# Linear attention and two feed-forward layers on one core: a Strassen-like slot opens the next slot's first product before it closes its own, and the written order is reckoned with other TensorE lengths

## The chip, the cores and the metric

The kernel runs on one core of one Trainium2 chip. Times are device microseconds (us) of that core, from the start to the end of one execution. Time before: median 829.05 us of three runs, which lie between 828.7 and 829.67. A difference under 0.2% (1.66 us) cannot be told from no change here.

## The reference

```python
kv  = einsum('bhsd,bhse->bhde', k, v)         # per batch and head: k^T v, 64 x 64
out = einsum('bhsd,bhde->bhse', q, kv)        # q, k, v: (4, 8, 576, 64)
x   = out / sqrt(mean(out*out, -1) + 1e-6) * g_norm
x   = x.transpose(0, 2, 1, 3).reshape(2304, 512)
x   = softplus(x @ w_in)  @ w_out            # moe:  w_in (512, 2048), w_out (2048, 512)
out = elu(x @ w_in2)      @ w_out2           # moe2: the same shapes
```

Everything is in float32.

## The kernel before

Each fp32 operand of a big product is split in two fp32r halves (`hi`, `lo`), and a product of two matrices is three matmuls (hi·hi, lo·hi, hi·lo). A matmul has 128 rows of contraction, 128 rows of output and 384 or 512 columns.

**Slots.** The 2304 tokens are six blocks of T = 384, taken in three pairs. The 2048 hidden columns are 16 chunks of 128, taken in four quarters. A layer has 4 quarters x 3 pairs x 2 chunk pairs = 24 slots; a slot makes the hidden values of one chunk pair for one pair of blocks (`slot_plain`, `slot_h`), and its results, split, are the tiles `G`. The product with `w_out` (`slot_out`, lines 986 to 988) runs in *pieces* of three matmuls, 384 wide in layer 0 and 512 wide in layer 1, for slots that are done; its banks are `acc`, and VectorE adds them up (`block_sum`, lines 570 to 584).

The first six slots multiply plainly (`plain_product`, line 759): four pairs of 6-matmul products. All later slots (`slot_h`) use seven products of six 384-wide matmuls (`product`, line 731) in place of eight. Products 1, 6, 7 and 4 add up in bank `A` (tag `h`, two banks). Between them ScalarE or VectorE copies what stands in `A` so far (`copy`, lines 819 and 821): `ca` after product 1, `cb` after 6, `cc` after 7, and the next product on `A` waits for its copy. Product 5 opens bank `B` (tag `m`, **one** bank), VectorE adds it into `cc` (`c22`, line 829), then product 3 closes `B`, and VectorE adds `B` into the copy `cb` (`c12`, line 829, `hj<-hj,B`), which frees the bank. Product 2 fills bank `C` (tag `o`) and is added into `ca` (`c11`). The activations follow (`slot_act`, lines 796 and 901 to 948).

**What sets the order.** All engines' instructions are written out in one order that the program works out when it is built. `Order.run` (lines 100 on) keeps strands, each with a key (how soon it is due) and a next step with a price per engine and what it needs; among the strands that could go next on an engine it takes the one with the smallest start time plus `min((key - least) * SLOPE, WAIT)`. The prices of TensorE's work come from `pe(n, passes)`. TensorE's slots and pieces are one strand, `main`, whose order inside a slot is the table `PRODUCTS`: numbers are products, words are counts of pieces. While nothing else of TensorE's is ready in the first slots, the strand `warm` (lines 1085 to 1100) issues 128 x 128 fp32 matmuls on an identity or a zero tile, which add nothing to the result and fill the time. An engine then runs its instructions strictly as written.

**The start.** Batches 0 to 3 of the attention (`kv` line 418, `po` line 481, transposes `pt` line 552) run on TensorE between the plain slots of the first 150 us; their inputs come by DMA, and VectorE, ScalarE and GpSimd work on them on the way to the split x. Weights are split on ScalarE and VectorE through the whole run (lines 282 to 357), and x tiles that are used again are written to DRAM (`spill`, line 701) and read back (line 688).

Of the kernel before, what the change touches and what calls it, by code (L numbers as in the profile page):

```python
# [1 line left out]

# [14 lines left out]
P = 128  # L17
# [7 lines left out]


def pe(n, passes=1):
    return passes * n * 0.4514 + 1


def act(n, psum=False):
# [11 lines left out]
class Order:  # L43
# [16 lines left out]

    COLD = 7300

    SLOPE = 60
    WAIT = 300
    EARLY_WAIT = 200
    def __init__(self):
        self.free = dict.fromkeys((PE, ACT, DVE, POOL, DMA), 0.0)
        self.marks = {}
# [99 lines left out]
def linear_attention_then_two_ffns(  # L168
# [27 lines left out]
    KC = DM // P  # L196
# [8 lines left out]
    NPAIR = NB // 2  # L205
    FP = QF // 2
    SLOTS = NQ * NPAIR * FP
    LAYERS = 2

    OPS = ((1, 6, 7, 5, 4, 2, 3), (1, 5, 6, 2, 7, 4, 3))  # L210
    PLAIN_OPS = (1, 2, 8, 4)
    EPS = 1e-6

# [11 lines left out]
    def ring(tag, n=1):  # L225
        return ("ring", tag, n)
# [176 lines left out]
    def kv_strand(b, c):  # L403
        n, r = 4 * 2 * D2, S - 4 * P
        yield ((DMA, dma(4 * n * P)),), room_free(KV_AT[b][c], b, c)
        t = acc_sb[KV_AT[b][c]]
        nc.sync.dma_start(t[:, :n], kv[b, c].rearrange("p n t d -> p (n t d)"))
        yield ((DMA, dma(2 * D2 * 4 * r)),), []
        nc.sync.dma_start(t[:r, n : n + 2 * D2], kv_rest[b, c].rearrange("p t d -> p (t d)"))
        old = [("po", x) for x in made_of(b - 2, c)] if b > 1 else []  # L410
        tag = "om"[c % 2]
        yield ((PE, 5 * 130),), [ring(tag), *old]
        p, p_h = psum(tag, f"kv{b}_{c}")
        for n in range(5):
            r = min(P, S - n * P)
            o = n * 2 * D2
            for i in range(2):
                nc.tensor.matmul(  # L418
                    p[i * D : (i + 1) * D, :D],
                    t[:r, o + i * D : o + (i + 1) * D],  # L420
                    t[:r, o + D2 + i * D : o + D2 + (i + 1) * D],
                    start=(n == 0),
                    stop=(n == 4),
                )
        mark("kvmm", b, c)
        f = kvf[b % 2][:, c, :]
        for i in range(2):
            s = slice(i * D, (i + 1) * D)
            e = yield ((ACT, act(D, True)), (DVE, dve(D))), []
            if e == ACT:  # L430
                nc.scalar.copy(f[s, s], p[s, :D])
            else:
                nc.vector.tensor_copy(f[s, s], p[s, :D])
        drop(p_h)
        mark("kv", b, c)
# [15 lines left out]
    def attention(nm):  # L451


        first = isinstance(nm, tuple)
        if first:
            j, c = nm
            products = [
                (b, c, slice(s, e), slice(i * D2, (i + 1) * D2), j * TT + i)
                for i in range(TT)
                for b, s, e in batches(j * TT + i)  # L460
            ]
            n = T
            x = acc_sb[j][:, c * T : (c + 1) * T]
            tag = "acc"
        else:
            j, o = divmod(nm, TT)
            products = [
                (b, c, slice(s, e), slice(c * D2, (c + 1) * D2), nm)
                for b, s, e in batches(nm)
                for c in range(NP)  # L470
            ]
            n = DM
            x = acc_sb[j].rearrange("p (c t) -> p c t", c=KC)[:, :, o * P : (o + 1) * P]
            tag = "acc" if j < 3 else "om"[nm % 2]
        h = n // D
        need = dict.fromkeys([("kv", p[0], p[1]) for p in products] + [("tile", p[4]) for p in products])

        yield ((PE, sum(pe(P, 4) for _ in products)),), [ring(tag), *need, *room_free(j, B, 0)]
        bank, po_h = psum(tag, f"po{nm}")
        for b, c, rows, cols, t in products:  # L480
            nc.tensor.matmul(  # L481
                bank[rows, cols], tile_q[t][0][:, c, rows], kvf[b % 2][:, c, :], start=True, stop=True
            )
        if first:
            drop(tile_q[products[0][4]][1])
        mark("po", nm)
        po = bank[:, :n]
        if not first:
            yield from late(nm, bank, po_h, x, tag)
            return  # L490
        yield ((ACT, act(n, True)),), [ring("e")]
        y, y_h = sbuf("e", 3, f"y{nm}", (P, 2, T))
        y = y.rearrange("p a b -> p (a b)")[:, :n]
        nc.scalar.activation(y, po, AF.Square, scale=D**-0.5)
        yield ((DVE, dve(n)),), [ring("small")]
        small, small_h = sbuf("small", 4, f"small{nm}", (P, 2, H))
        ms, r = (small[:, i, :h] for i in range(2))
        nc.vector.reduce_sum(ms, y.rearrange("p (h e) -> p h e", h=h), axis=AX.X)

        yield ((POOL, power(h)),), [("minus_half",)]  # L500
        root(r, ms)
        yield ((DVE, dve(n)),), []
        nc.vector.tensor_mul(
            y.rearrange("p (h e) -> p h e", h=h),
            po.rearrange("p (h e) -> p h e", h=h),
            r.unsqueeze(2).to_broadcast([P, h, D]),
        )
        drop(small_h)
        yield ((PE, n // P * 109),), [("ident",)]
        for i in range(n // P):  # L510
            s = slice(i * P, (i + 1) * P)
            nc.tensor.transpose(bank[:, s], y[:, s], ident)
        drop(y_h)
        yield ((ACT, act(n, True) + 90),), [("gn",)]
        nc.scalar.activation(x, po, AF.Copy, scale=gn)
        drop(po_h)
        mark("x", nm)
# [6 lines left out]
    def late(t, bank, po_h, x, tag):  # L524
# [20 lines left out]
        )  # L545
        drop(small_h)
        drop(po_h)
        yield ((PE, KC * 109),), [("ident",), ring(tag)]
        bank, po_h = psum(tag, f"pt{t}")
        for k in range(KC):  # L550
            s = slice(k * P, (k + 1) * P)
# [245 lines left out]
            drop(bank_h)  # L797
        yield from slot_parts(s, b, h, 2 * s + b)

    def slot_h(s, pieces):  # L800

        layer, q, p, f = slots[s]
        key = base(s)

        wide = s > FP and slots[s - FP][0] == 0
        k = {}

        def share(part):
            return {"all": 99, "half": 8 if wide else 6, "more": 3 if wide else 2, "one": 1, "two": 2}[part]

        def copy(name, tag, n, col):
            def strand():
# [21 lines left out]
            k[name] = psum(tag, f"{name}{s}", uses)  # L834
            return k[name][0]

        def some(n):
            yield from some_of(pieces, n)

        def first():  # L840
            yield from product(s, 1, lambda: open_("h", "A"), True, False, [ring("h")])
            chain[:] = [k["A"][0]]
# [6 lines left out]
        def seventh():  # L849
            yield from product(s, 7, k["A"][0], False, False, [("cb", s)])  # L850
            order.add(key - URGENT, copy("cc", "hk", 7, 1))

        def fifth():
            yield from product(s, 5, lambda: open_("m", "B"), True, False, [ring("m")])
# [12 lines left out]
        def third():  # L867
            yield from product(s, 3, k["B"][0], False, True, [("c22", s)])
            order.add(key - URGENT, add_to("hj", 1, *k["B"], "c12", []))
            order.add(key + H_KEY + 1, slot_act(s, 0, k["hj"], None))  # L870

        for step in PRODUCTS[layer]:
            if step in (1, 2, 3, 4, 5, 6, 7):
                yield from (first, second, third, fourth, fifth, sixth, seventh)[step - 1]()
            else:
                yield from some(share(step))
        if p == NPAIR - 1:
            for fc in (2 * f, 2 * f + 1):
                for h in w_t[layer, fc, 0][2:]:
                    drop(h)  # L880
            drop(wx_t[layer, 2 * f][1])

    def G_tiles(n, name):

# [83 lines left out]
    def slot_piece(layer, q, p, b, u, k, cut, acc, left):  # L968
# [29 lines left out]

    SUM_KEY = 0
    H_KEY = 2
    URGENT = 3
    X_LEAD = 3
    W_LEAD = 4
    W_LEAD2 = 8
    KV_KEY = (-20, -18, -5, 2)
    UNIT_KEY = (-19.9, -17.9, -9, -4, 4, 5)
    W_IN_FIRST = (-18.5, -11)
    W_OUT_FIRST = (-3, -1)  # L1010
    X_KEY = (-19, 2, 8)
    X_SUMS = (1.5, 9, 17)
    SPILL = 1
    WARM_SLOTS = 7
    FILLED = 8
# [2 lines left out]

    chain = []

    PRODUCTS = (
        (1, "more", 6, "more", 7, "one", 5, "more", 4, "one", 2, "more", 3, "two"),
        (1, 5, 6, 2, 7, "half", 4, 3, "all"),
    )

    class Pieces:
# [12 lines left out]
        def ready(self):  # L1039
            if not self:  # L1040
                return 0.0
            at = [order.when(n) for n in self.head[2]]
            return None if None in at else max(at)

        def take(self):
            if self:
# [8 lines left out]
    def some_of(pieces, n):  # L1055
        for _ in range(n):
            yield from one(pieces)
# [9 lines left out]
    def main():  # L1067
        groups = LAYERS * SLOTS // FP
        for g in range(groups):
            layer, q, p, _ = slots[FP * g]  # L1070
            for b in range(2):
                last = g == groups - 1 and b == 0
                pieces_of[FP * (g + 1) + (1 - b if g >= NPAIR else b)] = Pieces(slot_out(layer, q, p, b, last))
        for s in range(LAYERS * SLOTS + 2):
            if s:
                entry[0] = base(s)
            left = pieces_of.get(s, Pieces(iter(())))
            if s < FP * NPAIR:
                yield from slot_plain(s, left)
            elif s < LAYERS * SLOTS:  # L1080
                yield from slot_h(s, left)
            while left:
                yield from one(left)

# [124 lines left out]
```

## Time and profile before

| | before |
|---|---|
| median of 3 runs | 829.05 us |
| the profiled execution | 828.14 us |
| its span (first to last instruction) | 826.2 us |
| PE (TensorE matmul) busy | 819.5 us, 99% |
| PEld (weight loads, beside PE) | 773.9 us, 94% |
| DVE (VectorE) | 551.6 us, 67% |
| ACT (ScalarE) | 448.4 us, 54% |
| POOL (GpSimd) | 43.8 us, 5% |
| chain that ended last | PE 95%, ACT 2%, DVE 1%, POOL 1% |

A row of a timeline is: start, duration, engine, line, operation, output <- inputs, shape, count, and in brackets how long the engine had stood idle before it and what ended that. Matmuls overlap: the row of one lasts longer than the distance to the start of the next, which is the *pitch*, and the pitch is what a matmul costs in a row of matmuls. A tile's name is given without its numbers.

### The profile page before, as it was taken

The page shows a single profiled execution, that of the slowest core. Times are in us where ns is not written, and L with a number is a line of the kernel's source. Part 1 is how long each engine was busy: PE and PEld are TensorE (multiplying, and loading weights), DVE is VectorE, ACT ScalarE, POOL GpSimd, SP SyncE. Part 2 cuts the span into 40 slices and gives each one's busy share as a digit, 9 for nine tenths or more (in the row PEclk, how much of TensorE's full clock was granted, in tenths as well). Part 3 has the DMA queues.
Part 4 walks back from the last instruction along what each step waited for, and adds up shares of the span by engine and source line. Part 5 has one row for each costly group of instructions (what it writes and reads, how often), then busy time and mean ns, then how long its engine had stood idle before and what let it go on. Part 6 is the DMA issues. An engine that isn't in the chain of part 4 may idle for free.

```text
span 826.2 us, 12278 instructions
## 1 busy us (share of the span) xinstructions
PE 819.5 (99%) x4772; PEld 773.9 (94%) x4772; DVE 551.6 (67%) x906; ACT 448.4 (54%) x767; POOL 43.8 (5%) x47
## 2 busy tenths in 40 slices
PE   9999999999999999999999999999999999999998
PEld 8899999999999999999999998889889889889897
DVE  3787697354476565766399987767578766865444
ACT  4686785463255534544276777675364564563340
POOL 3442420000000000000000000000000000000000
PEclk9999999999999999999999999999999999999999
DMA  8988666774574674675644756673763763653713
GB/s 310 306 328 319 220 233 228 299 280 172 185 280 163 245 270 140 253 260 168 235 160 159 292 201 240 273 275 141 273 240 118 297 251 138 256 222 111 278 39 114
DMA packets 42537, 185.34 MB, mean 224 GB/s; under 512 B 4976, under 2 KB 6256, under 8 KB 42480
## 3 DMA queue, kind: packets, MB, share of 16 engines
q1 hardware_dynamic: 42480, 184.57, 60.8%
q8 instruction: 37, 0.61, 0.3%
q14 instruction: 20, 0.16, 0.1%
HBM read 146.80 MB, written 37.75 MB: 223 GB/s over the span
## 4 chain that ended last, share of the span: by engine, by line
PE 95%; ACT 2%; DVE 1%; POOL 1%; issue 0%; DVEq 0%
PE A L731 21%; PE acc L988 16%; PE acc L987 16%; PE acc L986 15%; PE B L731 10%; PE A L759 6%; PE C L731 5%; PE kv L418 2%; PE warm L1098 2%; PE po L481 1%; PE A L1098 1%; POOL small L522 1%; PE pt L552 1%; ACT acc_sb L570 0%; DVE x L693 0%
## 5 line engine op out<-in xcount | busy, mean ns | idle before, releaser
L986 PE MATMUL acc<-G,whi 128*128 128x384 f32 x384 | 128.7, 335 | 0.0
L988 PE MATMUL acc<-G,whi 128*128 128x384 f32 x384 | 128.3, 334 | 0.0
L987 PE MATMUL acc<-G,wlo 128*128 128x384 f32 x384 | 128.3, 334 | 0.0
L988 PE MATMUL acc<-wlo,G 128*128 128x512 f32 (+1 forms) x292 | 113.6, 389 | 0.0
L987 PE MATMUL acc<-whi,G 128*128 128x512 f32 (+1 forms) x292 | 113.5, 389 | 0.0
L986 PE MATMUL acc<-whi,G 128*128 128x512 f32 (+1 forms) x292 | 112.7, 386 | 0.0
L731 PE MATMUL A<-x,wx 128*128 128x384 f32 x504 | 101.3, 335 | 0.4 <-ACT hj L819 0.3
L731 PE MATMUL A<-x,whi 128*128 128x384 f32 x336 | 99.5, 337 | 0.4 <-ACT hk L796 0.4
L731 PEld LDWEIGHTS A<-x,wx 128*128 128x128 f32 x504 | 88.5, 188 | 1.4 <-ACT hj L819 1.4
L986 PEld LDWEIGHTS acc<-G,whi 128*128 128x128 f32 x384 | 72.1, 188 | 0.1
L987 PEld LDWEIGHTS acc<-G,wlo 128*128 128x128 f32 x384 | 72.1, 188 | 0.0
L988 PEld LDWEIGHTS acc<-G,whi 128*128 128x128 f32 x384 | 72.1, 188 | 0.0
L576 DVE TENSOR_TENSOR acc_sb<-acc_sb,acc 128x384 f32<-128x384 f32 (+1 forms) x108 | 62.1, 597 | 12.5 <-PE acc L988 12.5
L988 PEld LDWEIGHTS acc<-wlo,G 128*128 128x128 f32 x292 | 54.8, 188 | 11.2
L731 PEld LDWEIGHTS A<-x,whi 128*128 128x128 f32 x336 | 62.4, 188 | 2.5 <-ACT hk L796 0.8
L987 PEld LDWEIGHTS acc<-whi,G 128*128 128x128 f32 x292 | 54.8, 188 | 10.3
L986 PEld LDWEIGHTS acc<-whi,G 128*128 128x128 f32 x292 | 54.9, 188 | 10.2
L312 ACT CAST whi<-q 128x512 fp32r<-128x512 f32 x64 | 39.7, 620 | 41.7 <-DVE q L341 12.4
L819 ACT COPY hj<-A 128x384 f32<-128x384 f32 x56 | 26.9, 480 | 61.2 <-PE A L731 61.2
L316 DVE TENSOR_TENSOR wlo<-q,whi 128x512 fp32r<-128x512 f32 x64 | 44.0, 688 | 23.3 <-ACT whi L312 23.2
L829 DVE TENSOR_TENSOR hj<-hj,B 128x384 f32<-128x384 f32 x42 | 23.2, 553 | 53.0 <-PE B L731 53.0
L829 DVE TENSOR_TENSOR hk<-hk,B 128x384 f32<-128x384 f32 x42 | 23.3, 554 | 52.2 <-PE B L731 37.6
(169 smaller groups left out, 1604.1 us busy)
## 6 DMA issues: line engine op xcount, KB each, us to landing
x<-spill SPq DMA_DIRECT2D x126, 768.0 KB, 6.3
raw<-w SPq DMA_DIRECT2D x64, 512.0 KB, 6.5
spill<-x SPq DMA_DIRECT2D x42, 768.0 KB, 4.6
acc_sb<-kv SPq DMA_DIRECT2D x16, 512.0 KB, 5.6
q<-qt SPq DMA_DIRECT2D x18, 256.0 KB, 4.9
out<-o SPq DMA_DIRECT2D x17, 256.0 KB, 2.1
acc_sb<-kv_rest SPq DMA_DIRECT2D x16, 64.0 KB, 5.3
out<-o SPq DMA_DIRECT2D x2, 128.0 KB, 1.7
```

The costliest lines, as they stand in the source:

```text
L312: nc.scalar.copy(hi, q)
L316: nc.vector.tensor_sub(lo, q, f32(hi))
L418: nc.tensor.matmul(p[i * D : (i + 1) * D, :D], t[:r, o + i * D : o + (i + 1) * D], t[:r, o + D2 + i * D : o + D2 + (i + 1) * D], start=(n ...
L576: nc.vector.tensor_add(a, a, p)
L731: nc.tensor.matmul(bank[:, :T], w, x, start=start and i == 0, stop=stop and i == len(seq) - 1, skip_group_check=True,)
L759: nc.tensor.matmul(a[:, :T], w, x, start=half == 0 and i == 0, stop=half == 1 and i == len(seq) - 1, skip_group_check=True,)
L819: nc.scalar.copy(to, a[:, :T])
L829: nc.vector.tensor_add(to, to, bank[:, :T])
L986: nc.tensor.matmul(a, l[0], r[0], start=(u == 0), stop=False)
L987: nc.tensor.matmul(a, l[1], r[0], start=False, stop=False)
L988: nc.tensor.matmul(a, l[0], r[1], start=False, stop=(u == QF - 1))
L1098: nc.tensor.matmul((chain[0] if chain else p)[:, -P:], a, a, start=not chain, stop=not chain, skip_group_check=True)
```

## The change

There are three parts.

1. **Product 1 of the next slot comes early.** `slot_h` gives back its seven steps in place of running them, and `main` holds the steps of this slot and of the next. The table `STEPS` takes the place of `PRODUCTS`: a 1 there means the *next* slot's product 1, which now stands ahead of products 4 and 3 of this slot. The order of a slot's other products becomes 6, 5, 2, 7.
2. **One run of 512-wide pieces a slot.** In layer 1 a slot had two runs of pieces (`"half"` and `"all"`). Now it has one, of 6 pieces in even slots and 18 in odd ones; the pieces that an even slot leaves are kept and go ahead of the odd slot's (`Pieces.follow`).
3. **Other numbers for the order.** `pe` goes from 174.3 to 173.3 ns for 384 columns, from 232.1 to 226.6 for 512 and from 232.1 to 263.3 for the filler's four passes of 128; transposes, `kv`, the slopes, waits and keys change too. These numbers set the order alone.

```diff
 def pe(n, passes=1):
-    return passes * n * 0.4514 + 1
+    return passes * n / 2.4 + (13.3 if passes == 1 else 50)
...
-    SLOPE = 60
-    WAIT = 300
-    EARLY_WAIT = 200
+    SLOPE = 90.0
+    WAIT = 118.0
+    EARLY_WAIT = 190.0
...
-    OPS = ((1, 6, 7, 5, 4, 2, 3), (1, 5, 6, 2, 7, 4, 3))
+    OPS = ((1, 6, 5, 2, 7, 4, 3),) * 2
...
-        yield ((PE, 5 * 130),), [ring(tag), *old]
+        yield ((PE, 880),), [ring(tag), *old]
...
-    def slot_h(s, pieces):
+    def slot_h(s):
...
         def seventh():
             yield from product(s, 7, k["A"][0], False, False, [("cb", s)])
             order.add(key - URGENT, copy("cc", "hk", 7, 1))
+            if p == NPAIR - 1:
+                drop(wx_t[layer, 2 * f][1])
...
-        for step in PRODUCTS[layer]:
-            if step in (1, 2, 3, 4, 5, 6, 7):
-                yield from (first, second, third, fourth, fifth, sixth, seventh)[step - 1]()
-            else:
-                yield from some(share(step))
-        if p == NPAIR - 1:
...
+        return None, first, second, third, fourth, fifth, sixth, seventh
...
-    SUM_KEY = 0
-    H_KEY = 2
-    URGENT = 3
+    SUM_KEY = -1.52
+    H_KEY = 1
+    URGENT = 8
...
-    PRODUCTS = (
-        (1, "more", 6, "more", 7, "one", 5, "more", 4, "one", 2, "more", 3, "two"),
-        (1, 5, 6, 2, 7, "half", 4, 3, "all"),
+    STEPS = (
+        ((6, "4", 5, 2, "4", 7, "8", 1, 4, 3),) * 2,
+        ((6, 5, 2, 7, "6", 1, 4, 3), (6, 5, 2, 7, "18", 1, 4, 3)),
     )
...
+        def follow(self, other):
+            self.pieces = itertools.chain(self.pieces, other.pieces)
...
             left = pieces_of.get(s, Pieces(iter(())))
+            if kept:
+                kept.follow(left)
+                left, kept = kept, None
             if s < FP * NPAIR:
                 yield from slot_plain(s, left)
             elif s < LAYERS * SLOTS:
-                yield from slot_h(s, left)
+                if s == FP * NPAIR:
+                    now = slot_h(s)
+                    yield from now[1]()
+                for step in STEPS[slots[s][0]][s % FP]:
+                    if isinstance(step, str):
+                        yield from some_of(left, int(step))
+                    elif step > 1:
+                        yield from now[step]()
+                    elif s + 1 < LAYERS * SLOTS:
+                        then = slot_h(s + 1)
+                        yield from then[1]()
+                now = then
+                if slots[s][0] and s % FP == 0:
+                    left, kept = kept, left
             while left:
                 yield from one(left)
```

The first place is on TensorE, at the start of plain slot 1 (`A_0_0`, block 1's first product), with the attention and the filler ahead of it (`A_1_1` is the last bank of slot 0, onto which the filler multiplies the identity with `start` and `stop` off). Before:

```order
L1098 MATMUL A_1_1_647<-ident 128x128 x4
L481 MATMUL po_722<-kvf_69,q_466 128x128 x4
L481 MATMUL po_733<-kvf_69,q_499 128x128 x4
L1098 MATMUL A_1_1_647<-ident 128x128 x9
L759 MATMUL A_0_0_768<-x_0_0_1_299,whi_2_0_560 128x384
L759 MATMUL A_0_0_768<-x_0_0_1_299,wlo_2_0_589 128x384
```

and after:

```order
L760 MATMUL A_1_1_615<-x_0_0_4_557,whi_1_0_387 128x384 x2
L553 MATMUL pt_638<-ident,q_395 128x128 x4
L419 MATMUL kv_2_646<-acc_sb_75 64x64 x10
L553 MATMUL pt_661<-ident,q_395 128x128 x4
L760 MATMUL A_0_0_669<-x_0_0_1_289,whi_2_0_498 128x384
L760 MATMUL A_0_0_669<-x_0_0_1_289,wlo_2_0_522 128x384
```

Here the fillers ahead of slot 1 are gone and the `po` products of the next batch come later. Counted over the whole order, there are 70 rows' worth of fillers before (42 ahead of the first plain product, 28 behind it) and 34 after (32 and 2); one such matmul is two records in the trace, so 140 records before and 68 after.

The second place is on TensorE too, in layer 1, around product 3, which closes bank `B` (the only one of its tag). Before, the last products of a slot (`A_5788`, `B_5799`) are followed by its 18 matmuls on `acc` (the first three are shown) and then by the next slot's product 1, so product 5 reopens bank `B` 24 matmuls behind product 3:

```order
L731 MATMUL A_5788<-x_1_1_4_5630,whi_7_0_5384 128x384 x2
L731 MATMUL B_5799<-x_1_1_3_5653,whi_7_0_5384 128x384
L731 MATMUL B_5799<-x_1_1_3_5653,wlo_7_0_5394 128x384
L731 MATMUL B_5799<-x_1_1_3_5653,whi_7_0_5384 128x384
L731 MATMUL B_5799<-x_1_1_3_5653,wlo_7_0_5394 128x384
L731 MATMUL B_5799<-x_1_1_3_5653,whi_7_0_5384 128x384 x2
L986 MATMUL acc_1_0_0_0_5840<-whi_6_1_5574,G_0_5666 128x512
L987 MATMUL acc_1_0_0_0_5840<-whi_6_1_5574,G_0_5666 128x512
L988 MATMUL acc_1_0_0_0_5840<-wlo_6_1_5579,G_0_5666 128x512
```

and after, where `A_5867` and `B_5902` are the next slot's banks:

```order
L732 MATMUL A_5712<-x_1_1_4_5623,wlo_7_0_5286 128x384
L732 MATMUL A_5712<-x_1_1_4_5623,whi_7_0_5280 128x384 x2
L732 MATMUL B_5759<-x_1_1_3_5649,whi_7_0_5280 128x384
L732 MATMUL B_5759<-x_1_1_3_5649,wlo_7_0_5286 128x384
L732 MATMUL B_5759<-x_1_1_3_5649,whi_7_0_5280 128x384
L732 MATMUL B_5759<-x_1_1_3_5649,wlo_7_0_5286 128x384
L732 MATMUL B_5759<-x_1_1_3_5649,whi_7_0_5280 128x384 x2
L732 MATMUL A_5867<-x_1_2_6_5778,wx_4_5106 128x384 x6
L732 MATMUL B_5902<-x_1_2_5_5803,wx_4_5106 128x384 x6
```

The next slot's product 1 now stands ahead of these rows, its product 6 follows product 3 at once, and product 5 (`B_5902`) comes only 6 matmuls behind product 3 of the last slot (`B_5759`).

The third place is on VectorE at the same point of a layer 1 slot, around `c12`, the add `hj<-hj,B` that frees that bank; `c`, `r`, `raw`, `q` are steps of the split of a weight tile. Before:

```order
L295 ISA q_9_0_5782<-c_9_0_5781,r_9_0_5795 128x1024
L288 TENSOR_SCALAR c_10_0_5861<-c_10_0_5861 128x512
L290 SCALAR_TENSOR_TENSOR c_10_0_5861<-raw_10_0_5741,c_10_0_5861 128x512
L295 ISA q_10_0_5862<-c_10_0_5861,r_10_0_5867 128x1024
L829 TENSOR_TENSOR hj_5808<-hj_5808,B_5799 128x384
L920 SCALAR_TENSOR_TENSOR hk_5844<-e_1_5889,A_5788 128x384
L925 SCALAR_TENSOR_TENSOR hk_5844<-e_1_5889,hk_5844 128x384
```

and after:

```order
L359 TENSOR_TENSOR wx_10_6105<-t_1_10_6107,wx_10_6105 128x256
L289 TENSOR_SCALAR c_10_1_6143<-c_10_1_6143 128x512
L291 SCALAR_TENSOR_TENSOR c_10_1_6143<-raw_10_1_5757,c_10_1_6143 128x512
L826 TENSOR_TENSOR hj_5990<-hj_5990,B_6016 128x384
L296 ISA q_10_1_6144<-c_10_1_6143,r_10_1_6167 128x1024
L818 COPY hj_6165<-A_6150 128x384
```

Ahead of `c12` stand steps of a weight's split in both; behind it now comes another step of the split and a copy of the next slot's bank `A`, where there were steps of the slot's own activation.

## Rows read from the trace of the kernel before

**Rows 1.** Windows: busy us (count) by engine, granted clock, DMA share, GB/s.

```profile
25.00:57.00 32.00, 32.00 (x316) 29.08 (x315) 25.63 (x43) 24.26 (x50) 16.50 (x16) 1.00 0.92 322
150.58:431.80 281.22, 281.22 (x1622) 281.22 (x1623) 168.27 (x295) 132.50 (x225) 0.00 (x0) 1.00 0.60 217
560.00:826.00 266.00, 263.13 (x1318) 236.79 (x1316) 171.13 (x278) 122.96 (x200) 0.00 (x0) 1.00 0.50 189
```

**Rows 2.** Line 1098, the filler: records, min/median/max ns, first and last start.

```profile
L1098 PE MATMUL A<-ident x56: 271/275/377, 31.6 to 56.3; 128*128 128x128 f32 x56
L1098 PE MATMUL warm<-kvf x42: 275/326/582, 1.4 to 13.2; 128*128 128x128 f32 x42
L1098 PE MATMUL warm<-ident x42: 275/275/377, 15.3 to 23.9; 128*128 128x128 f32 x42
```

**Rows 3.** Timeline of TensorE, runs of filler and the start of slot 1.

```profile
1.44 4.21 PE L1098 MATMUL warm<-kvf 128*128 128x128 f32 x18 [1.44 <-DVE kvf L1113]
...
54.44 2.17 PE L1098 MATMUL A<-ident 128*128 128x128 f32 x18
56.57 0.44 PE L759 MATMUL A<-x,whi 128*128 128x384 f32 x1
```

**Rows 4.** Timeline of ScalarE, the last softplus of slot 0.

```profile
56.02 0.50 ACT L796 ACTIVATE hk<-A 128x384 f32<-128x384 f32 x1
```

**Rows 5.** Waits of TensorE in the first 151 us: total, times, longest.

```profile
PE pt L552 <- DVE q L541: 0.9, 2, 0.6
PE A L731 <- ACT hk L796: 0.4, 1, 0.4
```

**Rows 6.** Timeline of TensorE: two layer 1 slots begin; two 512-wide pieces.

```profile
572.90 0.33 PE L731 MATMUL A<-x,whi 128*128 128x384 f32 x1
...
588.47 0.33 PE L731 MATMUL A<-x,whi 128*128 128x384 f32 x1
...
811.26 0.39 PE L986 MATMUL acc<-whi,G 128*128 128x512 f32 x1
...
816.02 0.39 PE L986 MATMUL acc<-whi,G 128*128 128x512 f32 x1
```

**Rows 7.** Timeline, layer 1, TensorE and ScalarE: first and last stops at product 7.

```profile
497.51 0.51 PE L731 MATMUL C<-x,whi 128*128 128x384 f32 x2
497.79 0.47 ACT L819 COPY hj<-A 128x384 f32<-128x384 f32 x1
...
498.31 1.32 PE L731 MATMUL A<-x,wx 128*128 128x384 f32 x6 [0.29 <-ACT hj L819]
...
529.66 0.51 PE L731 MATMUL C<-x,whi 128*128 128x384 f32 x2
530.24 0.97 PE L731 MATMUL A<-x,wx 128*128 128x384 f32 x4
```

**Rows 8.** Timeline: product 3 and the add that frees its bank; product 5.

```profile
429.58 0.51 PE L731 MATMUL B<-x,whi 128*128 128x384 f32 x2
...
431.64 0.55 DVE L829 TENSOR_TENSOR hj<-hj,B 128x384 f32<-128x384 f32 x1
...
432.24 0.45 PE L731 MATMUL B<-x,wx 128*128 128x384 f32 x1
...
584.00 0.51 PE L731 MATMUL B<-x,whi 128*128 128x384 f32 x2
...
584.55 0.55 DVE L829 TENSOR_TENSOR hj<-hj,B 128x384 f32<-128x384 f32 x1 [1.85 <-PE B L731]
```

**Rows 9.** The page, part 6: reloads of x, KB each, median us to landing.

```profile
x<-spill SPq DMA_DIRECT2D x126, 768.0 KB, 6.3
```

**Rows 10.** Timeline: from a slot's last product on A to its G.

```profile
583.51 0.49 ACT L911 ACTIVATE e<-A 128x384 f32<-128x384 f32 x1 [2.26 <-PE A L731]
...
586.81 0.82 ACT L946 CAST G<-hk 128x768 fp32r<-128x768 f32 x1
...
589.28 0.95 DVE L948 TENSOR_TENSOR G<-hk,G 128x768 fp32r<-128x768 f32 x1
```

More of the change, by code (lines that the diff above doesn't have):

```diff
@@ L1 @@
+import itertools
 from contextlib import ExitStack
@@ L508, in attention @@
         drop(small_h)
-        yield ((PE, n // P * 109),), [("ident",)]
+        yield ((PE, n // P * 90),), [("ident",)]
         for i in range(n // P):
@@ L547, in late @@
         drop(po_h)
-        yield ((PE, KC * 109),), [("ident",), ring(tag)]
+        yield ((PE, KC * 90),), [("ident",), ring(tag)]
         bank, po_h = psum(tag, f"pt{t}")
@@ L798, in plain_act @@
         yield from slot_parts(s, b, h, 2 * s + b)
-    def slot_h(s, pieces):
+    def slot_h(s):
         layer, q, p, f = slots[s]
         key = base(s)
-        wide = s > FP and slots[s - FP][0] == 0
         k = {}
-        def share(part):
-            return {"all": 99, "half": 8 if wide else 6, "more": 3 if wide else 2, "one": 1, "two": 2}[part]
         def copy(name, tag, n, col):
@@ L835, in open_ @@
             return k[name][0]
-        def some(n):
-            yield from some_of(pieces, n)
         def first():
@@ L870, in third @@
             order.add(key + H_KEY + 1, slot_act(s, 0, k["hj"], None))
-        for step in PRODUCTS[layer]:
-            if step in (1, 2, 3, 4, 5, 6, 7):
-                yield from (first, second, third, fourth, fifth, sixth, seventh)[step - 1]()
-            else:
-                yield from some(share(step))
-        if p == NPAIR - 1:
[L878 to L881, printed above, removed]
+            if p == NPAIR - 1:
+                for fc in (2 * f, 2 * f + 1):
+                    for h in w_t[layer, fc, 0][2:]:
+                        drop(h)
+        return None, first, second, third, fourth, fifth, sixth, seventh
     def G_tiles(n, name):
@@ L997, in slot_piece @@
             order.add(base(s) + SUM_KEY, block_sum(layer, q, 2 * p + b, i, w0, w1, *acc.pop(k)))
-    SUM_KEY = 0
-    H_KEY = 2
-    URGENT = 3
+    SUM_KEY = -1.52
+    H_KEY = 1
+    URGENT = 8
     X_LEAD = 3
[L1005 to L1008, printed above, removed]
+    W_LEAD = 5
+    W_LEAD2 = 7
+    KV_KEY = (-19.9, -18, -7, 2)
+    UNIT_KEY = (-19.9, -17.9, -9, 0, 2.4, 1.1)
     W_IN_FIRST = (-18.5, -11)
-    W_OUT_FIRST = (-3, -1)
-    X_KEY = (-19, 2, 8)
-    X_SUMS = (1.5, 9, 17)
+    W_OUT_FIRST = (0.9, 2.5)
+    X_KEY = (-12, 3.5, 7.5)
+    X_SUMS = (9.0, 2.9, 16.5)
     SPILL = 1
```

1 line of the change is left out of this document (added).

## The prediction, as it went on record before the run

> **What bounds the kernel now.** I read the windows by stage first, then the groups of the filler, the waits and the timelines around the few stops. In the windows [rows 1] TensorE is busy 281.22 of 281.22 us from 150.58 to 431.80, the slots of layer 0 behind the plain ones: 1622 matmuls at 281.22 / 1622 = 0.1734 us, which is the pitch of a 384-wide one. There is nothing to gain there but fewer matmuls, and both orders issue the same products and pieces. In layer 1 from 560 us on, 263.13 of 266.00 us are busy, the end of the run included. So only three things can move the time: matmuls that compute nothing, stops of TensorE, and what a matmul costs by its neighbours. VectorE is busy 171.13 us of those 266, two thirds, and 25.63 of 32 us from 25 to 57: it has room, but not at every moment.
>
> Those matmuls that compute nothing are the filler [rows 2]: 56 + 42 + 42 = 140 records, up to 56.3 us. Their pitch is 0.112 us, from (2.17 - 0.28) / 17 in the run at 54.44 [rows 3], with 0.28 the length of one [rows 2].
>
> **The change part by part.**
>
> *Fillers: -8.1, of which +1.5 comes back.* The order has 36 filler rows fewer, that is 72 records: 72 x 0.112 = 8.06 us. Ten of the rows stood ahead of the first plain product and 26 behind it. They filled time in which nothing else was ready, so the question is what is ready now. The 18 records at 54.44 end where slot 1 starts, at 56.57 [rows 3]; that slot waited for a bank which the last softplus of slot 0 gave back at 56.02 + 0.50 = 56.52 [rows 4]. ScalarE's written order had that softplus late, not the data, and after the change the activations have a smaller key (`H_KEY` 2 to 1) and slot 1's product stands ahead of the later attention. Going through the first 60 us of the new order by hand, with row durations, the first plain product comes 1.8 us earlier and slot 1 some 10 us earlier, with attention work moved behind it. Bounds: 0 comes back if all of it was the order's doing, 8.06 if the start is bound by data: VectorE 80%, ScalarE 76% and the DMA engines 92% busy from 25 to 57 [rows 1]. By hand the engines keep up with small slack, so I take 1.5. The stops that this stage has already, 0.9 and 0.4 us [rows 5], may go or stay: between 0 and -1.3, and I take 0.
>
> *Runs of 512-wide pieces: -1.4.* A layer 1 slot lasts 588.47 - 572.90 = 15.57 us [rows 6]. By pitch it is 42 x 0.1734 + 36 x 0.2267 = 15.44, with 0.2267 from (816.02 - 811.26) / 21 in a long run, without stops between. The 0.13 us too many lie at the changes from 384 to 512 wide, of which the slot has two runs: 0.065 for one. The order has 44 such runs before and 23 after: 21 x 0.065 = 1.4. Bounds: 0 if the surplus goes by matmuls and not by runs, 1.4 if by runs.
>
> *Product 7's stops in layer 1: -1.25.* Product 7 comes one product, 1.04 us, behind product 6, and the copy `cb` has to fit in between. Where ScalarE is late it doesn't: matmuls at 497.51 x2 end by pitch at 497.86, the copy at 498.26, and product 7 starts at 498.31, 0.45 late and with 0.11 more for the first matmul (1.32 in place of 5 x 0.173 + 0.33 = 1.20) [rows 7]. There are three such stops, the last from 530.01 to 530.24: 0.45 + 0.23 + 0.23 + 3 x 0.11 = 1.25. In the new order products 5 and 2 stand between 6 and 7, 2.08 us, and 4 and 3 between 1 and 6, in place of 5 alone: 2.08 for 1.04. A copy as late as the latest here then fits. Bounds: 0 and -1.25.
>
> *Bank B: +2.0.* This is the added wait. Product 5 reopens the bank that `c12` frees, and now comes one product behind product 3 (the sixth) where it had 18 matmuls of pieces and product 1 between, 4.1 + 1.04 us. The row at 584.00 ends by pitch at 584.35; `c12` runs from 584.55 to 585.10 [rows 8]. A wait is released 0.05 us later (copy 498.26, product 498.31 [rows 7]). Product 5 could start at 584.35 + 1.04 = 585.39, so the slack is 0.24 us if VectorE is free. Behind product 5 all of TensorE's order is queued, and behind `c12` on VectorE the next copies and splits. Lower bound: `c12` is 0.20 behind product 3 in nearly every layer 1 slot before, as in this row, and then the cost is 0. Upper bound: at 431.64 it came 1.71 us behind (429.58 + 0.35 = 429.93), held by other VectorE work, and there product 5 did wait, until 432.24 [rows 8]. That happened in 3 of the 18 `slot_h` slots of layer 0; one such place would cost 1.71 - 0.24 + 0.11 = 1.58, and 23 slots at that rate 23 x 3/18 x 1.58 = 6.1. In the new order a step of a weight's split stands directly ahead of `c12` in 13 of the 24 slots. There is about 1 VectorE operation per us (278 in 266 us [rows 1]), say of 0.7 us, and the written order lets a less urgent one begin if that is 118 ns ahead of `c12` or more (`WAIT`). One that begins 0.12 to 0.46 us ahead overruns the slack: a chance of 0.34, by 0.17 on average and 0.11 for the restart, 23 x 0.34 x 0.28 = 2.2. I take 2.0, nearer to the layer 1 row than to the others.
>
> The trace's own example is the one at 431.64: the add was ready and stood behind others. The Trainium skill states this as a rule (PSUM — Partial Sum Buffer, Engine vs sequencer instructions): the queues of ScalarE, VectorE and GpSimd are strictly first in, first out. By that rule an urgent key helps only when the order is written, and a late step in front would hold every product 5 behind it; the trace agrees with its 1.71 us.
>
> *Layer 0, reloads, tail: +0.3.* In layer 0 four pieces stand between 6 and 5, so product 5 has 1.04 + 12 x 0.173 = 3.1 us behind product 3, more than the 1.71 + 0.55 of the worst row [rows 8]: 0. The early product 1 takes its x reloads with it on SP's queue. The tightest are those of products 4 and 3 in an even layer 1 slot, whose buffer comes free one such slot earlier, 7.3 + 18 x 0.227 = 11.4 us against 6.3 to landing [rows 9]: 0, and a stop of a few us at each only if the queue is twice as slow. At the end, the last pieces need the G of the last slot's product 4. It takes 0.2 us to the first activation (as `c12` takes), from there 586.81 + 0.82 - 583.51 = 4.12 to the cast and 0.95 for the last step [rows 10]: 5.3 us, where the new order needs it 5.1 us behind product 4; with the restart +0.3. Bounds 0 and 2.0, since the last step waited 589.28 - 587.63 = 1.65 for VectorE here.
>
> **Sum.** -8.1 + 1.5 - 1.4 - 1.25 + 2.0 + 0.3 = -6.95 us. The profiled execution took 828.14, of which 826.2 are the span and 1.94 lie around it; it gives 821.2, and the median of the runs stands 0.91 above it: 822.1.
>
> **Rivals.**
>
> *The fillers come back as waits (828.3).* If the start is bound by its data, 36 fillers only become as much idle time: -8.1 + 8.1 - 1.4 - 1.25 + 2.0 + 0.3 = -0.45, 828.6; with half of bank B's price 827.6; I put it at 828.3. This is also the case in which the first part of the change does nothing. For it: DMA 92% busy [rows 1], two stops for `q` from VectorE even with the fillers [rows 5]. Against it: the filler at 54.44 waited for ScalarE's order [rows 4]. 0.13.
>
> *Bank B at nearly every slot (839.0).* One mechanism, on the slower side: an operation of VectorE as long as the last step of G, 0.95 us [rows 10], starts just ahead of `c12` in each slot. Then product 5 waits 0.95 - 0.24 + 0.11 = 0.82, 23 x 0.82 = 18.9, and the time is 829.05 - 8.95 + 18.9 = 839.0. It is slower than before by over 0.2% from (8.95 + 1.66) / 23 = 0.46 us a slot on. Against it: the 0.20 of layer 1, and two thirds of use. 0.08.
>
> *TensorE slows where it idles (825.7).* The first 18 fillers, right behind 1.44 us of idle time, took 4.21 us, (4.21 - 0.58) / 17 = 0.213 a record, against 0.112 later [rows 2, 3]: 18 x 0.10 = 1.8 us. The granted clock reads 1.00 in every window [rows 1], 2.4 GHz, but this pitch is that of the lower level. If real stops in the new start let that happen twice: 822.1 + 2 x 1.8 = 825.7. Against it: the longest stop now is 0.6 us [rows 5] and matmuls behind it keep their pitch. 0.04.
>
> A rule of the Trainium skill speaks against taking fillers out (TensorE: Matmul & The Clock Gate, Why this matters for your kernels): idle gaps between bursts of matmuls bring the clock down. By that rule the new start would pay the rival's 1.8 us each time; no row of this trace shows a fall, only the slow beginning.
>
> **How the numbers follow.** The forecast, 822.1, has 0.70, with a range of its own of 817 to 826: down by 1.5 (nothing comes back), 2.0 (bank B costs nothing), 0.3 and 1.3 (old stops go), up by some 4 if half of the fillers or the layer 0 rate of bank B comes true. The rivals have 0.13, 0.08 and 0.04, and 0.05 is left for what I don't see, half on either side. A difference under 0.2%, 1.66 us, can't be told from none. Faster: 0.70 + 0.04 + 0.03 + a quarter of the first rival = 0.80; same: 0.11; slower: 0.09. The range of 8 in 10 goes from 816.0 to 828.4, which takes in the first rival and leaves the second out.
>
> **What would show it.** In the changed profile: records of line 1111 (the filler's new line) down to 68, and the first slot of seven products, ahead of which the new order has four pieces, 2.1 us, more, starting at 150.58 - 6.6 + 2.1 = 146.1; at 152.7 all fillers came back as waits. Layer 0 gapless at 0.1734 a matmul. In layer 1 no wait on copies of A, and the idle time of TensorE ahead of `B` on `hj<-hj,B`: some 0.1 us a slot for the forecast, from 0.46 on it decides against it. A slot pair of layer 1 lasting 2 x 15.57 - 0.13 us shows the runs. The prediction is wrong if the start is as long as before or product 5 stops in most slots.

## The result, and the profile after

The changed kernel takes 817.23 us (median of four runs, 816.9 to 817.82) against 828.88 us for the kernel before on the same chip: a ratio of 0.9863, 95% interval 0.9852 to 0.9875. The forecast was 822.1 us, 6.95 us less; it came out 11.65 us less, inside the range. The profiled execution took 816.9 us, its span 815.1.

The page of the changed kernel, part 1, and its windows, cut where its stages change (columns as in [rows 1]):

```profile
PE 808.2 (99%) x4700; PEld 764.6 (94%) x4700; DVE 562.1 (69%) x927; ACT 434.7 (53%) x746; POOL 44.0 (5%) x47
```

```profile
25.00:57.00 32.00, 32.00 (x300) 28.97 (x299) 26.91 (x45) 24.70 (x52) 16.22 (x16) 1.00 0.96 341
...
144.27:420.00 275.73, 275.73 (x1592) 275.73 (x1592) 171.37 (x294) 126.58 (x219) 0.00 (x0) 1.00 0.63 223
...
560.00:815.00 255.00, 252.05 (x1264) 226.75 (x1263) 161.73 (x266) 113.38 (x183) 0.00 (x0) 1.00 0.52 190
```

The first slot of seven products starts at 144.27 in place of 150.58, with four pieces more ahead of it. Layer 0 is as gapless as before, 275.73 / 1592 = 0.1732 us a matmul. Next the filler, line 1111 now, and all waits of TensorE in the run (total, times, longest):

```profile
L1111 PE MATMUL warm<-kvf x32: 275/399/583, 1.4 to 12.1; 128*128 128x128 f32 x32
...
L1111 PE MATMUL warm<-ident x32: 275/275/377, 14.4 to 23.3; 128*128 128x128 f32 x32
...
L1111 PE MATMUL A<-ident x4: 275/275/275, 34.9 to 35.2; 128*128 128x128 f32 x4
```

```profile
PE warm L1111 <- DVE kvf L1126: 1.4, 1, 1.4
PE kv L419 <- DMA acc_sb<-kv: 0.9, 2, 0.5
PE po(0, 0)_164 L482 <- DMA q<-qt: 0.8, 2, 0.5
PE pt L553 <- DVE q L542: 0.5, 1, 0.5
```

Of 140 filler records [rows 2] 68 are left, four of them behind the first plain product. The waits for ScalarE's `hk` [rows 5] and for the copy `hj` [rows 7] are gone, and no wait for bank B has come. What is new, 0.9 + 0.8 us, are waits for the attention's first loads, where ten filler rows stood.

In layer 1, TensorE and VectorE around product 3 (a timeline):

```profile
575.92 0.33 PE L732 MATMUL A<-x,whi 128*128 128x384 f32 x1
...
590.14 0.51 PE L732 MATMUL B<-x,whi 128*128 128x384 f32 x2
...
590.49 1.20 PE L732 MATMUL A<-x,wx 128*128 128x384 f32 x6
590.69 0.56 DVE L826 TENSOR_TENSOR hj<-hj,B 128x384 f32<-128x384 f32 x1 [0.78 <-PE B L732]
...
591.53 1.20 PE L732 MATMUL B<-x,wx 128*128 128x384 f32 x6
...
606.93 0.33 PE L732 MATMUL A<-x,whi 128*128 128x384 f32 x1
```

Product 3 ends by pitch at 590.49, `c12` runs from 590.69 to 591.25, and product 5 opens bank B at 591.53, straight behind product 6, with no wait. The add is 0.20 us behind product 3, as in the row at 584.00 [rows 8]. The two slots from 575.92 to 606.93 take 31.01 us, which is 2 x 15.57 - 0.13, as forecast.

To compare kernels I split the trace by TensorE's work. *Dead time of the start* is the start of the first slot of seven products, less the matmuls ahead of it at their pitches (0.1733 us for 384 columns, 0.112 for a record of 128, 0.045 for one of 64; no filler counted). *Surplus behind* is the same from there to the last matmul (0.2267 for 512 columns). Both are worked out from all TensorE records of one profiled execution and are good to some 0.1 us; the median is that of all runs, so the two need not move alike.

| kernel | median us | filler records | first slot of 7 at | dead time of the start | surplus behind |
|---|---|---|---|---|---|
| before | 828.88 | 140 | 150.58 | 26.6 | 4.8 |
| changed | 817.23 | 68 | 144.27 | 18.2 | 2.1 |
| numbers alone | 819.53 | 68 | 144.24 | 18.2 | 4.6 |
| slots and pieces alone | 827.09 | 140 | 151.71 | 27.7 | 2.7 |
| lengths alone | 823.85 | 98 | 147.54 | 22.5 | 4.2 |
| lengths, slope, waits | 820.10 | 86 | 144.69 | 20.2 | 3.3 |
| keys of the start alone | 824.71 | 104 | 148.06 | 24.1 | 3.8 |
| H_KEY alone | 828.30 | 134 | 150.51 | 26.5 | 4.0 |
| before, 28 fillers out | 829.88 | 84 | 150.86 | 26.9 | 4.8 |
| changed, no filler | 820.57 | 0 | 149.37 | 23.3 | 2.1 |
| changed, two runs | 819.63 | 68 | 146.99 | 20.9 | 3.2 |
| changed, long runs | 834.49 | 68 | 144.01 | 17.9 | 19.6 |
| changed, 5 ahead of 6 | 841.01 | 68 | 145.42 | 19.3 | 25.3 |
| changed, c12 late | 840.37 | 68 | 144.77 | 18.7 | 25.0 |

From before to changed, 8.4 us are gone from the start and 2.7 behind it: 11.1, the difference of the two profiled spans (826.2 and 815.1).

### The profile page after: what moved, and what is told of

It is laid out like the page before. It is cut to its first block, busy times and chain, and to the rows that moved or that the text cites. A ratio compares the mean times of both kernels' runs of the same rounds, so it can differ in the third digit from the quotient of the medians.

```text
span 815.1 us, 12155 instructions
## 1 busy us (share of the span) xinstructions
PE 808.2 (99%) x4700; PEld 764.6 (94%) x4700; DVE 562.1 (69%) x927; ACT 434.7 (53%) x746; POOL 44.0 (5%) x47
## 4 chain that ended last, share of the span: by engine, by line
PE 96%; DMA 2%; SPq 1%; POOL 0%; DVE 0%; issue 0%; ACT 0%
PE A L732 22%; PE acc L978 16%; PE acc L979 16%; PE acc L977 16%; PE B L732 11%; PE A L760 6%; PE C L732 5%; DMA acc_sb<-kv 2%; PE po L482 1%; PE kv L419 1%; PE pt L553 1%; POOL small L523 0%; SPq L449 0%; SPq L408 0%; SPq L410 0%; PE po(1, 1)_389 L482 0%
## 5 line engine op out<-in xcount | busy, mean ns | idle before, releaser
L732 PE MATMUL A<-x,whi 128*128 128x384 f32 x336 | 92.5, 335 | 0.0
L816 ACT COPY hj<-A 128x384 f32<-128x384 f32 x50 | 23.9, 478 | 119.6 <-PE A L732 119.4
L826 DVE TENSOR_TENSOR hj<-hj,B 128x384 f32<-128x384 f32 x42 | 23.3, 554 | 63.9 <-PE B L732 63.7
L979 PEld LDWEIGHTS acc<-wlo,G 128*128 128x128 f32 x292 | 54.8, 188 | 11.1
L978 PEld LDWEIGHTS acc<-whi,G 128*128 128x128 f32 x292 | 54.8, 188 | 11.1 <-DVE G L939 0.4
L317 DVE TENSOR_TENSOR wlo<-q,whi 128x512 fp32r<-128x512 f32 x64 | 44.0, 688 | 21.2 <-ACT whi L313 20.9
L283 ACT ACTIVATE c<-raw 128x512 f32<-128x512 f32 x64 | 42.8, 668 | 27.4 <-DVE q L296 13.9
```

What stands on the lines that cost most here:

```text
L283: nc.scalar.activation(c.bitcast(F32), high_f, AF.Copy, scale=2.0**-112)
L317: nc.vector.tensor_sub(lo, q, f32(hi))
L732: nc.tensor.matmul(bank[:, :T], w, x, start=start and i == 0, stop=stop and i == len(seq) - 1, skip_group_check=True,)
L816: nc.scalar.copy(to, a[:, :T])
L826: nc.vector.tensor_add(to, to, bank[:, :T])
L978: nc.tensor.matmul(a, l[1], r[0], start=False, stop=False)
```

## The experiments

The theory after the result: the start is shorter because the written order is another (the numbers), layer 1 because the stops at product 7 are gone and the runs are halved (the slots), and bank B costs nothing. The rivals stand with each run.

**The numbers alone, and the slots alone.** The first is the kernel before with the hunks `pe` to `X_SUMS`, the second the changed kernel with them taken back:

```diff
 # numbers alone: PRODUCTS, slot_h and main as before
+    return passes * n / 2.4 + (13.3 if passes == 1 else 50)
+    SLOPE = 90.0 ... X_SUMS = (9.0, 2.9, 16.5)
 # slots and pieces alone: STEPS, slot_h, follow and main as changed
-    return passes * n / 2.4 + (13.3 if passes == 1 else 50)
-    SLOPE = 90.0 ... X_SUMS = (9.0, 2.9, 16.5)
```

> The kernel before with the new prices, slopes, waits and keys alone; slots, table of products and pieces as before. Its order has 34 filler rows, as the changed kernel has. Theory (the shorter start comes from the numbers, some 8 us, and the slots give the other 2.7): 820.5 us, with the first slot of seven products near 144 to 146 us in place of 150.6, and layer 1 slots of 15.57 us as before. Rival (the early product 1 is what shortens the run, the numbers only fit it): 827 to 829.

> The changed kernel with all prices, slopes, waits and keys put back to those of before; only the early product 1 and the one run of pieces are left. 70 filler rows. Theory: layer 1 without stops at product 7 and with half the runs, -2.7, the start as before: 826.2 us; bank B free in time as in the changed kernel. Rival 1 (the gain is in the slots): 818 to 820. Rival 2 (it was the new, more urgent keys that kept c12 at 0.20 us behind product 3, and with the old ones product 5 waits): 828 to 832, with stops at B.

The numbers alone give 819.53, ratio 0.9885 (0.9872 to 0.9899); the slots alone 827.09, 0.9973 (0.9964 to 0.9982). The differences, 9.7 and 2.1 us against 829.19 for the kernel before, run beside them, add up to the change's 11.7. By the table the numbers take 8.4 us from the start and nearly nothing behind it, the slots 2.1 behind it. In the profile of the slots alone the start is 1.1 us longer, with one wait of 1.9 us for the load of `q`, and its runs spread from 825.82 to 828.64, so that sum is good to about 1 us. With the old keys `c12` was still 0.20 us behind product 3 in 40 of 42 slots, and product 5 did not wait for it, so the second rival of the slots falls.

**The fillers.** Left out behind the first plain product of the kernel before, and altogether in the changed one; all other instructions stand where they stood:

```diff
 # before
-            if entry[0] < base(WARM_SLOTS):
+            if entry[0] < base(WARM_SLOTS) and not chain:
 # changed
-            if entry[0] < base(WARM_SLOTS):
+            if False:
```

> The kernel before without the 28 filler rows behind the first plain product (56 records, 6.3 us); nothing else in any engine's order moves. Theory (they filled time in which the written order of ScalarE and the data gave TensorE nothing, and that order is what the change mends): idle time takes their place, 829 us, slot 1 at 56 to 57 us as before. Rival (they are too many, and stood in the way of work that was ready): up to 6.3 us faster, 822.6.

> The changed kernel without any filler (68 records, 7.6 us); no other instruction moves. Theory: the fillers only filled idle time, so the time by work and data stays at 817.2, but TensorE then idles through most of the first 15 us, and its clock is seen at the lower level later than now, in the first products: 818 to 820, with a granted clock under 1.00 between 5 and 25 us, as one run of the kernel with two runs showed (0.50 from 10 to 15 us, first product 2.7 us late). Rival (the clock does not matter here): 817.2. Rival (the fillers stood in the way): below 817.

Before without its 28 takes 829.88, ratio 1.001 (1.0 to 1.0019): idle time takes their place. Here is what stands where [rows 3] had 18 records (a timeline of that kernel's TensorE):

```profile
52.85 2.05 PE L481 MATMUL po<-kvf,q 128*128 128x128 f32 x16 [0.94 <-ACT kvf L431]
56.87 0.45 PE L759 MATMUL A<-x,whi 128*128 128x384 f32 x1 [1.97 <-ACT hk L796]
```

Nothing stands between the two rows before the bank comes free: the last softplus of slot 0 starts at 56.31 there, as late as in [rows 4]. So fewer fillers alone are worth nothing. In the changed kernel the last 68 are even worth 3.3 us: without them it takes 820.57, ratio 0.9899 (0.9883 to 0.9914) to before, and the clock is seen to fall (windows, columns as in [rows 1]):

```profile
20.00:24.00 4.00, 2.85 (x30) 2.43 (x29) 2.48 (x6) 3.47 (x7) 2.38 (x4) 1.00 1.06 343
24.00:28.00 4.00, 3.68 (x30) 2.75 (x30) 3.74 (x7) 3.22 (x8) 1.25 (x1) 0.64 1.03 335
```

TensorE is idle 1.15 of 4 us, then the granted clock of 24 to 28 us is 0.64, part of it at 1.2 GHz, and the first plain product starts at 28.46 instead of 24.56. The column does not show all of it. Here are six `po` matmuls without the fillers, then the same six in the changed kernel (timelines):

```profile
18.52 1.65 PE L482 MATMUL po(0, 2)_223<-kvf,q 128*128 128x128 f32 x6
```

```profile
15.56 0.94 PE L482 MATMUL po(0, 2)_240<-kvf,q 128*128 128x128 f32 x6
```

At 18.52 the column reads 1.00, but records of 128 columns stand 0.213 us apart there, from 12 to 21 us, as the first fillers before did at 1.44 [rows 3]; in the changed kernel they stand 0.112 apart from 6 us on. So without fillers TensorE still works at the pitch of the lower level there. That is not the whole price: the run with a mean clock of 1.0 takes 819.37, still 1.55 us above the slowest of the changed kernel.

**Which of the numbers.** All four are the kernel before with some of them:

```diff
 # keys of the start: W_LEAD, W_LEAD2, KV_KEY, UNIT_KEY, W_OUT_FIRST, X_KEY, X_SUMS as changed
 # H_KEY
-    H_KEY = 2
+    H_KEY = 1
 # lengths, slope, waits: pe, kv 880, transposes 90, SLOPE, WAIT, EARLY_WAIT as changed
 # lengths: the same without SLOPE, WAIT, EARLY_WAIT
```

> The kernel before with the keys of the start alone (the leads of the weights, the keys of the attention's units, of w_out and of x and its sums); H_KEY, URGENT, prices, slopes and waits as before. 52 filler rows, 14 of them behind the first plain product (28 before, 2 after). Theory (the keys decide what is ready for TensorE between 25 and 144 us, and idle time goes as the fillers do): half to most of the 6 us of the numbers, 823 to 826, the first slot of seven products 3 to 5 us earlier. Rival (it is the activations' key, the prices and the waits, as the prediction had it with H_KEY): 828 to 829.

> The kernel before with H_KEY 1 in place of 2 and nothing else: the prediction's own reason for the shorter start, that ScalarE's order had the last softplus of slot 0 late. 67 filler rows, 25 of them behind the first plain product (28 before). Prediction's reason: 3 to 6 us faster. Theory now (the keys of the start make 4.5 us, the prices and waits the rest, H_KEY next to nothing): 828 to 829.

> The kernel before with the new prices of TensorE's work and the new slope and waits, all keys as before. 43 filler rows, 7 behind the first plain product. Theory (what the keys alone left of the numbers' 9.7 us, 5.2, comes from here): 824 us, less of it in the start than with the keys if the two overlap. Rival (prices and waits only matter together with the keys): 828 to 829.

> The kernel before with the new lengths of TensorE's work alone (matmuls, transposes, kv); slope, waits and all keys as before. 49 filler rows, 17 behind the first plain product. Theory (the start is shorter where the order knows how long TensorE takes, and the waits are a smaller matter): 822 to 824, work and data apart from it as before, that is 3 to 5 us less of dead time before the first slot of seven products (26.6 us before, 20.2 with lengths and waits). Rival (the lengths do nothing without the shorter waits, which let an operation go first only by 118 ns in place of 300): 828 to 829.

Keys 824.71 (ratio 0.9945, 0.9933 to 0.9957), H_KEY 828.3 (0.9995, 0.9986 to 1.0005), lengths with slope and waits 820.1 (0.9903, 0.9888 to 0.9918), lengths alone 823.85 (0.9942, 0.9928 to 0.9955). Lengths make 4.9 us, the slope and waits 3.6 more, the keys of the start 4.5 by themselves; all keys together, with `H_KEY`, `SUM_KEY` and `URGENT`, add only about 1 on top of lengths, slope and waits (819.53). `SUM_KEY` and `URGENT` were not tried alone, nor the slope without the waits. I had expected 824 of the lengths with slope and waits: they overlap with the keys far more than I thought.

The prediction's reason, that the activations' key held slot 1, is true of slot 1 and of nothing more. With `H_KEY` alone, slot 1 starts at 50.13 in place of 56.57 [rows 3]; its 25th matmul follows at 62.06 (timeline):

```profile
50.13 0.42 PE L759 MATMUL A<-x,whi 128*128 128x384 f32 x1
...
62.06 0.42 PE L759 MATMUL A<-x,whi 128*128 128x384 f32 x1
```

In the kernel before, the 25th is this one:

```profile
62.54 0.42 PE L759 MATMUL A<-x,whi 128*128 128x384 f32 x1
```

So 6.4 us of lead are down to 0.5 half a slot later, with pieces, attention and fillers in between, and of the 56 filler records behind the first plain product 50 are left.

**The runs of 512-wide pieces.**

```diff
-        ((6, 5, 2, 7, "6", 1, 4, 3), (6, 5, 2, 7, "18", 1, 4, 3)),
+        ((6, "6", 5, 2, 7, "6", 1, 4, 3),) * 2,        # two runs a slot
+        ((6, 5, 2, 7, 1, 4, 3), (6, 5, 2, 7, "24", 1, 4, 3)),   # long runs
```

> The changed kernel with two runs of six pieces in every layer 1 slot (6, six pieces, 5, 2, 7, six pieces, 1, 4, 3) in place of one run; 34 filler rows as in the changed kernel; bank B has 4.1 us more. Theory (a change from 384 to 512 wide costs 0.065 us a run): 46 runs in place of 23, +1.5, 818.7 us. Rival (the surplus goes by matmuls, and the 2.5 us that layer 1 lost were its stops): 817.2. If bank B still cost something in the changed kernel, this one would lose it: below 817.

> The changed kernel with all pieces of two layer 1 slots in the odd one (even slots none, odd ones 24): 12 runs of 512-wide pieces in place of 23. Theory (0.065 us a run, no new waits): -0.7, 816.5 us. Rival (the activations of two slots and the adds of 24 pieces come in bursts, and the tiles G are held longer): stops in front of the pieces or of product 6, 818 to 822.

With two runs, TensorE from the first 512-wide matmul on has 3.23 us over the pitch in place of 1.76: 1.47 us for 22 more runs (45 in the trace, 23 in the changed kernel), 0.067 each, as the slot rows had it [rows 6]. The median, 819.63 (ratio 0.9888, 0.9874 to 0.9901), is 0.9 above the forecast. The profiled run, the slowest of the four with 820.83, shows what can add to it: the first plain product came 2.7 us later, at a clock that fell (windows):

```profile
5.00:10.00 5.00, 3.05 (x31) 2.12 (x29) 0.00 (x0) 0.41 (x2) 0.00 (x0) 0.87 0.98 304
10.00:15.00 5.00, 5.00 (x35) 4.54 (x36) 1.11 (x2) 0.90 (x3) 1.61 (x2) 0.50 1.04 333
```

Of the two runs whose mean clock is 1.0, one takes 818.98 and the other 819.76, so the clock does not explain all of the 0.9.

The long runs take 834.49 (1.0063, 1.0042 to 1.0084), where I had expected 816.5: the rival came true, and far beyond its 818 to 822. TensorE's waits there:

```profile
PE A L732 <- ACT hj L816: 6.8, 3, 3.3
PE B L732 <- DMA x<-spill: 3.3, 6, 1.6
```

Without pieces between two slots' products, copies come late: product 6 stops until 434.08 and until 501.65, over 3 us each time. In later slots product 3 waits for its reloaded x. Around the two long stops the granted clock falls to 0.50 (435.6 to 439 and 500.5 to 507.2 us). The waits are 10.1 of the 17.5 us by which the surplus grew; how the rest divides was not worked out.

**Bank B, twice.** First product 5 straight behind product 3; then `c12` at the least urgent key:

```diff
-        ((6, 5, 2, 7, "6", 1, 4, 3), (6, 5, 2, 7, "18", 1, 4, 3)),
+        ((5, 6, 2, 7, "6", 1, 4, 3), (5, 6, 2, 7, "18", 1, 4, 3)),
 # c12 late
-            order.add(key - URGENT, add_to("hj", 1, *k["B"], "c12", []))
+            order.add(key + URGENT, add_to("hj", 1, *k["B"], "c12", []))
```

> The changed kernel with product 5 ahead of product 6 in layer 1, so that product 5 follows product 3 of the last slot at once; the copy after product 6 has 1.04 us in place of 2.08. It prices bank B. Theory (one bank, freed 0.20 + 0.55 + 0.05 us behind product 3, then a slow first matmul, 0.11): 0.91 us a slot, 23 slots, +20.9: 838 us, all of it as idle time ahead of B, released by VectorE. Rival (the release is slower than the one copy row showed, or VectorE is late behind its queue): 842 or more. Rival (TensorE reopens the bank without waiting for the add to end): 817.

> The changed kernel with c12, the add that frees bank B, put at the least urgent key of VectorE (key + 8 in place of key - 8). Theory now (the written order knows when product 3 ends to a few ns, since TensorE never stops in layer 1, and a key is worth at most 118 ns, so VectorE is seldom busy there): c12 0.20 us late in most slots, 817 to 818. The prediction's reckoning (an operation of 0.7 us begins at any time ahead of it): stops of 0.1 to 0.5 us at product 5 in a third of the slots or more, 819 to 822.

The first takes 841.01 (1.0143, 1.013 to 1.0156), 23.8 us more than the changed kernel; I had forecast 20.9. One of its 23 places:

```profile
590.01 0.51 PE L732 MATMUL B<-x,whi 128*128 128x384 f32 x2
...
590.56 0.56 DVE L826 TENSOR_TENSOR hj<-hj,B 128x384 f32<-128x384 f32 x1 [2.46 <-PE B L732]
...
591.17 1.14 PE L732 MATMUL B<-x,wx 128*128 128x384 f32 x5 [0.65 <-DVE hj L826]
```

590.36 by pitch, the add from 590.56 to 591.12, the product at 591.17: 0.81 and 0.11 for the restart, in 20 of 23 places exactly, 0.86 to 1.09 in the others. That is 0.94 on average or 21.6 us; 1.5 us more is a stop at product 7, whose copy again had 1.04 us, and the rest lies in the start. So the price and the release after 0.05 us hold, and with them the slack of 0.24 us, which is worked out from them.

The second takes 840.37 (1.0144, 1.0129 to 1.0159); I had expected 817 to 818, and that theory falls. The stops are not spread over the slots but stand at the switch of the layers. VectorE and TensorE there (a timeline):

```profile
427.78 0.51 PE L732 MATMUL B<-x,whi 128*128 128x384 f32 x2
...
428.13 1.20 PE L732 MATMUL A<-x,wx 128*128 128x384 f32 x6
428.16 0.96 DVE L694 TENSOR_TENSOR x<-acc_sb,x 128x768 fp32r<-128x768 f32 x1
...
429.05 0.69 DVE L317 TENSOR_TENSOR wlo<-q,whi 128x512 fp32r<-128x512 f32 x1
...
430.61 0.96 DVE L694 TENSOR_TENSOR x<-acc_sb,x 128x768 fp32r<-128x768 f32 x1 [0.87 <-ACT x L666]
...
431.49 0.95 DVE L939 TENSOR_TENSOR G<-hk,G 128x768 fp32r<-128x768 f32 x1
...
432.36 0.68 DVE L356 TENSOR_TENSOR wx<-t,wx 128x512 fp32r<-128x512 f32 x1
432.96 0.55 DVE L826 TENSOR_TENSOR hj<-hj,B 128x384 f32<-128x384 f32 x1
...
433.56 0.62 PE L732 MATMUL B<-x,wx 128*128 128x384 f32 x2 [4.23 <-DVE hj L826]
```

The add is ready at 428.3, stands behind five operations on the next layer's x, G and weights (one of which waits for ScalarE), and product 5 stops for 4.39 us. Four such places, from 411 to 488, stop TensorE for 14.9 us, and the clock falls behind them (0.74 from 445 to 451). From 510 on the same key leaves `c12` at 0.20 us in all slots but two.

## Why the prediction was right, term by term

*Fillers, -8.1 with +1.5 back: -6.6 forecast, -8.4 measured.* Ahead of the first plain product ten filler rows, 2.2 us, went, but it starts at 24.56, only 0.4 earlier, where by hand I had 1.8: 1.8 us came back there, 0.9 + 0.8 as the new waits for loads. Behind it the dead time fell by 8.0 us, more than the 5.8 of its 26 rows, since stops went too, two of those in [rows 5] among them, which I had put at 0. So it is chance that the 8.4 in all are about what the fillers had filled. Slot 1 was right by hand: it starts at 47.20, 9.4 us earlier. That the order held TensorE, and not the data, was right, as the same instructions in another order show. The reason was too narrow: `H_KEY` moves slot 1 and not the end, and the time came from the lengths with which the order is reckoned, the slope and waits, and the keys of the start. Of the lengths, a batch's `kv` matmuls were reckoned at 650 ns and now at 880, and they take 0.88 us (45.91 to 46.79 in the changed kernel); the filler's went from 232 to 263 ns, away from its 224. Which of the lengths does it wasn't tried.

*Runs, -1.4: -1.4,* 21 runs at the 0.067 us of the kernel with two runs. *Product 7, -1.25:* no such wait is left; the numbers alone kept a stop there (0.98 us at 442), the slots alone none.

*Bank B, +2.0: failed.* It is the step that was mis-sized: it cost nothing, and the 0.34 us of the old stop at 432 [rows 8] went too. The chance reckoning took VectorE's operations as coming at any time. But the order is written with TensorE's pitch in hand, TensorE hardly stops in layer 1, and next to no operation begins that would run into the add: 0.20 us in 39 of 42 slots. That reason is argued; what is seen is the 0.20 us, with the least urgent key too from 510 us on. One slot was lucky: at 450.85, where product 3 ended, the add came 1.08 us behind it, and pieces left from layer 0 stood ahead of the next product 5. The row of layer 1 was the one to follow; that of layer 0, 1.71 us, had adds of pieces in front, since pieces stood directly ahead of product 3; in the new table products 1 and 4 stand between. The rival of 839 us needs VectorE overfull, and the less urgent key shows that place: it is the switch of the layers, not every slot. There the steps in front of the add cost up to 4.4 us a place.

*Tail, +0.3: +0.23,* two long distances in the last pieces (799.24 to 799.59 to 799.92 in place of 0.227 each). The reloads cost nothing, as forecast.

The clock, a rival at 0.04, did not decide, but four kernels above (no filler, two runs, long runs, `c12` late) show that it is real. A new stop of 0.24 us stands at 443, in front of a piece whose bank VectorE gave back late. The sum of the terms behind the start is -1.25 - 0.34 - 1.4 + 0.23 + 0.24 = -2.5, against -2.7 by the table. In the prediction the first rival's terms add up to -0.35, not -0.45; the forecast does not rest on it.

## What to carry to other kernels

Where a filler stands, taking it out tells whether it or the order costs the time: here nothing came of fewer fillers until the order changed, and then 8.4 us came, of which the fillers had filled a part. In this kernel a wait that is added with a slack of a quarter of a microsecond cost nothing where the releasing queue was seldom full, and 2.7 to 4.4 us at each of four places around the switch of the layers, once its release had lost its urgent key; look for such places rather than average the load. Price each such wait from the row of the place in which it will stand.

## What the runs showed of the hardware that I had not expected

The granted clock of TensorE fell in the start of kernels with stops there, to 0.50 of 2.4 GHz from 10 to 15 us in the profile with two runs, with 1.95 us of idle time in 5 to 10 us, and to 0.64 from 24 to 28 us in the one without fillers; the changed kernel, idle 1.33 us from 5 to 10, kept 1.00. In the kernel before without its 28 fillers, eight of eleven runs have a mean clock of 0.996 to 0.998 and take 829.0 to 831.9 us, and three have 1.0 and take 828.3 to 828.8. The kernel before, run 54 times beside the experiments, was below 0.999 once (831.05 us): fillers that compute nothing still keep its runs alike.
